# Another filling of TensorE's early gaps, another path for u, and another written order, in an attention-then-feed-forward kernel

## The chip, the cores and the metric

The kernel runs on one core of one Trainium2 chip. Times are device microseconds (us) of whole executions of the program; the traces are single executions taken by the hardware profiler. The engines are named as in the profile: PE is TensorE (PEld its weight loads), ACT is ScalarE, DVE is VectorE, POOL is GpSimd, SP is SyncE, which here does nothing but start transfers (DMAs). A name with a q, such as SPq, is the engine's instruction queue.

## The reference

Two layers follow one another. The first is a linear attention with a decaying state, for 4 batches, 8 heads, 768 time steps and 48 values per head; the second is a feed-forward block without a nonlinearity.

```
for t in range(S):                                   # S = 768
    cur   = einsum('bhd,bhe->bhde', u * k_t, v_t)
    y_t   = einsum('bhd,bhde->bhe', r_t, state + cur)
    state = w_t[..., None] * state + einsum('bhd,bhe->bhde', k_t, v_t)
x   = y as (B*S, H*D)                                # 3072 x 384
out = ((x @ w1) * (x @ w2)) @ w3 @ w_out             # w1, w2: 384 x 1024; w3: 1024 x 1024; w_out: 1024 x 384
```

Inputs and output are float32; the matrix products run in bfloat16.

## The kernel before, in words

**Attention.** The 768 steps of each batch are cut into 6 chunks of 128 steps, which makes 24 chunks, numbered n = 0 to 23. `load(n)` brings w, k, r and v of a chunk from HBM, four transfers of 192 KB on SP's queue, into tiles with 8 buffers each. `att(n)` lists the steps of a chunk. `ln` (ACT) takes the logarithm of w; `cs` (two matmuls) forms cumulative sums in PSUM; `ex` (ACT) takes exponentials; `krt` (DVE) scales k and r by them; `tr` and `trs` transpose the result, with PE and an ACT copy for chunks 0 to 10, with a transposing DMA on SP's queue for chunks 11 to 23 (`kr_dma=11`). `vb` turns v into bfloat16; `kv` (PE), `pc`, `ts`, `st`, `sb` carry the state to the next chunk. `m` (PE) forms the 128 by 128 products per head, `mb` (DVE) masks them. `uk1`, `uk2` (POOL), `ds` (DVE) and `yd` (POOL) make the term with u. `y` (PE) and `yb` (DVE) make the output; `yt` (PE) and `xt` (ACT) lay it down transposed in the tile xT.

**u.** `ld_u` loads the 384 values of u into one row; `ub` is a float32 matmul of a row of ones with it, so that all 128 rows hold u; `uc` copies that to the tile u_bc, which `uk1` of every chunk reads.

**Feed-forward.** Chunks are gathered into blocks of 1 to 4 (`blocks`), 512 columns at most. For block j and each eighth fi of the 1024 columns, `a{j}.{fi}` and `b{j}.{fi}` are three matmuls each, `as` (ACT) copies a out of PSUM and `ab` (DVE) multiplies. The matrix w3 @ w_out is computed on the chip: `wt` transposes an eighth of w3 on PE, `wm` multiplies it with w_out. `o{j}.{t}` is then eight matmuls per chunk, `os` copies it out, `st` stores it. The weights arrive in seven pieces by POOL's queue (w1.0, w2.0, w1.1, w2.1, wo, w3.0, w3.1), each issued when the step named in `triggers` is done; w3.0 and w3.1 are needed by the first and the fifth `wt`.

**The order.** All steps are handed to a planner (`Plan`). It keeps a list of costs of its own, lets each engine take the ready step that can start first, breaks ties by a rank (the place in the list, shifted by `nudge`), and writes out one fixed order per engine; each engine runs its instructions strictly in that order. `lead` and `every` say how far the attention chunks stand ahead of the feed-forward parts in the list, `early` how many blocks' a and b stand ahead of the w3 part. The planner also notes where PE would stand idle before 30 us by its own times, and `keep_busy` puts matmuls of a zero tile (`busy`) ahead of the step there; they write to a PSUM bank that the step overwrites.

In the profile nearly all instructions carry line 186, the helper that records them, so they are found by their tiles.

Of the kernel before, what the change touches and what calls it, by code (L numbers as in the profile page):

```python
# [12 lines left out]

NEVER = 999
TUNE = dict(
    blocks=[1, 2, 3, 3, 3, 4, 4, 4],
    early=1,
    triggers=["uk20", "uk11", "uk21", "uk22", "uk22", "uk22", "uk22"],
    lead=5, every=4.0,
    v_act=5, s_act=NEVER, d_pool=NEVER, y_dma=NEVER, kr_dma=11, ahead=2.0, fill=30, nudge={}, st_act=5,  # L20
)


class Plan:
# [133 lines left out]
    def run(self):  # L158
        windows = []
        for _ in range(6):  # L160
            order, new, start, end = self._pass(windows)
            if new == windows:
                break
            windows = new
        self.start, self.end = start, end
        self.fill, at = {}, 1.2
        for n in order:
            if self.steps[n]["eng"] == "PE" and start[n] < TUNE["fill"]:
                gap = start[n] - at - 0.15
                self.fill[n] = max(0, int(gap / (0.43 if start[n] < 9 else 0.22)))  # L170
                at = start[n] + self.steps[n]["length"]
        for n in order:
            self.steps[n]["fn"]()

# [16 lines left out]
def kernel(  # L191
# [20 lines left out]
    pe, act, dve, pool, sp = (InOrder(tc, e) for e in (nc.tensor, nc.scalar, nc.vector, nc.gpsimd, nc.sync))  # L212
# [3 lines left out]
    C = 128  # L216
# [35 lines left out]
    u_bc = consts.tile([C, H, D], F32)  # L252
    u_row = consts.tile([1, DM], F32)
    ones_r = consts.tile([1, C], F32)
    busy = consts.tile([C, TB], BF)
# [34 lines left out]
    plan = Plan()  # L290
    plan.buffers(w_in=NIN, kr_in=NIN, v_in=NIN, lw=NS, krt=NS, v_bf=3, uk=2, ds=2, yd=3,
                 trs=3, mbf=2, ts=2, st=2, sb=NS, y_bf=3, a_sb=3, o_sb=3, xT=3, abT=3, w3T=2, f=3)
    T = {}

    def keep_busy(step, t):
        for _ in range(plan.fill.get(step, 0)):
            pe.matmul(t, lhsT=busy[:, 0:C], rhs=busy, start=True, stop=True)

    def pair(step):
        t = (g01, g23)[plan.found[step] // 2]  # L300
        keep_busy(step, t[:, 0, :])
        return t

    def bank(step):
        i = plan.found[step]
        t = (g01, g23, g4)[i // 2][:, i % 2, :]
        keep_busy(step, t)
        return t
# [4 lines left out]
    def load(n):  # L313
        b, c = divmod(n, NC)

        def src(ap):
            return ap[b, :, c * C:(c + 1) * C, :].rearrange("h t d -> t h d")

        def ld_w():
            T["w_in", n] = inp.tile([C, H, D], F32, tag="w_in", name="w_in")  # L320
            sp.dma_start(T["w_in", n], src(w))

        def ld_k():
            T["kr_in", n] = inp.tile([C, 2, H, D], F32, tag="kr_in", name="kr_in")
            sp.dma_start(T["kr_in", n][:, 0], src(k))

        def ld_r():
            sp.dma_start(T["kr_in", n][:, 1], src(r))

        def ld_v():  # L330
            T["v_in", n] = inp.tile([C, H, D], F32, tag="v_in", name="v_in")
            sp.dma_start(T["v_in", n], src(v))

        plan.add(f"ld_w{n}", "SP", 0.57, ld_w, take=["w_in"], rows=1024)
        plan.add(f"ld_k{n}", "SP", 0.57, ld_k, take=["kr_in"], rows=1024)
        plan.add(f"ld_r{n}", "SP", 0.57, ld_r, needs=[f"ld_k{n}"], rows=1024)
        plan.steps[f"ld_r{n}"]["needs"] = []
        plan.add(f"ld_v{n}", "SP", 0.57, ld_v, take=["v_in"], rows=1024)
# [191 lines left out]
    def ffn_ab(j, fi):  # L530
# [4 lines left out]
        def half(nm, w_):  # L535
            t = T[nm, j, fi] = ps_f.tile([P, TB], F32, tag="f", name=nm)
            keep_busy(f"{nm}{j}.{fi}", t)
            for di in range(DI):
                pe.matmul(t[:, 0:N], lhsT=w_[:, di, fi * P:(fi + 1) * P], rhs=T["xT", j][:, di, 0:N],
                          start=(di == 0), stop=(di == DI - 1))  # L540
# [66 lines left out]
          free=[f"wm{fi}"])  # L607


    load(0)  # L610
    plan.add("ld_u", "SP", 0.5, lambda: sp.dma_start(u_row, u.rearrange("h d -> (h d)")[None, :]), rows=20)

    def ub():
        T["ub"] = bank("ub")[:, 0:DM]
        pe.matmul(T["ub"], lhsT=ones_r, rhs=u_row, start=True, stop=True)

    plan.add("ub", "PE", 0.9, ub, needs=["ld_u"], bank=1, lag=0.3)
    plan.add("uc", "ACT", 0.45, lambda: act.copy(u_bc.rearrange("t h d -> t (h d)"), T["ub"]),
             needs=["ub"], free=["ub"])
    for n in range(1, NU):  # L620
        load(n)
# [2 lines left out]
    for g in range(2):  # L624
        for nm, dst, ap in (("w1", w1_bf, moe_w1), ("w2", w2_bf, moe_w2)):
            cols = slice(g * FH * P, (g + 1) * FH * P)
            pieces.append((f"{nm}.{g}", dst[:, :, cols], ap[:, cols], 2.8))
    pieces.append(("wo", wo_bf, moe_w_out, 6.0))
    for g in range(FI // W3G):
        rows = slice(g * W3G * P, (g + 1) * W3G * P)  # L630
# [24 lines left out]
    lead, every = TUNE["lead"], TUNE["every"]  # L655
# [38 lines left out]
```

## Time and profile before

| what | us |
|---|---|
| 13 runs, median | 186.53 |
| 13 runs, lowest and highest | 183.35, 189.33 |
| the profiled execution, whole time | 183.84 |
| its span, first to last instruction | 182.1 |
| PE busy within the span | 169.3 |
| DVE, ACT, POOL busy | 126.4, 107.2, 90.1 |

The span is what the trace shows; 1.74 us of the profiled execution's 183.84 us lie around it. The profiled execution is among the fastest of the runs, 2.69 us below their median. A line of a timeline gives start, duration, engine, line, operation, output<-input, shape and count; in brackets stands how long the engine was idle before and what ended that. Matmuls overlap in the pipeline, so durations of several matmuls in one line can overlap with the next line's; the time that a group takes from PE is the distance between starts.

### The profile page before, as it was taken

To read this page: it belongs to the slowest core of one execution; us is meant where nothing else is said; L and a number is where in the kernel's file an instruction comes from. 1 tells how busy PE (TensorE), PEld (TensorE's weight loads), DVE (VectorE), ACT (ScalarE), POOL (GpSimd) and SP (SyncE) were. 2 spreads that over 40 slices of the span, in tenths; PEclk is the share of its full clock that TensorE was granted. 3 is DMA by queue.
4 is the path that set the end of the run, shared out by engine and by line. 5 is a ranking of instruction groups with operands and counts; after the bars stand their busy time and mean duration, and the time that the engine had idled before them with its cause. 6 is when DMAs were issued, how large, how long until landed. Compare 5 with 4: busy or idle time off the path is not lost.

```text
span 182.1 us, 4449 instructions
## 1 busy us (share of the span) xinstructions
PE 169.3 (93%) x1658; PEld 101.5 (56%) x1667; DVE 126.4 (69%) x220; ACT 107.2 (59%) x220; POOL 90.1 (49%) x136
## 2 busy tenths in 40 slices
PE   5996898878999998999999999999999999999992
PEld 1443465755676665665666666565556544554451
DVE  7265664654687985898799969958996798804510
ACT  3355534741567886978857675776666666345431
POOL 4167998700536793759674663476265636000000
PEclk9999999999999999999999999999999999999999
DMA  6999999999999999999989999999999997131013
GB/s 117 190 187 204 220 207 173 197 204 205 181 199 166 195 171 224 206 175 203 197 195 205 152 238 212 157 223 244 189 203 230 213 214 102 30 130 43 4 50 123
DMA packets 120744, 31.76 MB, mean 174 GB/s; under 512 B 114065, under 2 KB 119698, under 8 KB 120722
## 3 DMA queue, kind: packets, MB, share of 16 engines
q1 hardware_dynamic: 115298, 24.65, 81.3%
q0 software_dynamic: 3696, 4.46, 14.5%
q10 hardware_dynamic: 1728, 2.36, 3.8%
q8 instruction: 13, 0.21, 0.5%
q14 instruction: 9, 0.07, 0.1%
HBM read 27.79 MB, written 4.72 MB: 179 GB/s over the span
## 4 chain that ended last, share of the span: by engine, by line
PE 70%; DMA 11%; issue 6%; POOL 6%; DVE 4%; ACT 1%; POOLq 0%; ACTq 0%
PE g L186 19%; PE o_ps L186 17%; PE a L186 14%; PE b L186 13%; DMA w_bf<-in_moe_w_dram 9%; PE wm L186 5%; DMA trs<-krt 3%; POOL uk L186 2%; PE wt L186 2%; POOL sbd L186 1%; POOL w_bf L186 1%; DVE mbf L186 1%; ACT trs L186 1%; POOL v_bf L186 1%; DVE krt L186 1%
## 5 line engine op out<-in xcount | busy, mean ns | idle before, releaser
L186 PEld LDWEIGHTS <-w_bf 128*128 128x128 bf16 x448 | 37.9, 97 | 26.8 <-DMA w_bf<-in_moe_w_dram 1.8
L186 DVE TENSOR_TENSOR abT<-a_sb,b 128x384 bf16<-128x384 f32 (+3 forms) x64 | 34.8, 551 | 14.0 <-ACT a_sb L186 7.2
L186 ACT COPY a_sb<-a 128x384 f32<-128x384 f32 (+3 forms) x64 | 30.6, 479 | 20.2 <-PE a L186 18.0
L186 PE MATMUL a<-xT,w_bf 128*128 128x384 bf16 (+3 forms) x187 | 41.1, 324 | 0.8 <-ACT a_sb L186 0.2
L186 PE MATMUL b<-xT,w_bf 128*128 128x384 bf16 (+3 forms) x191 | 41.4, 325 | 0.1
L186 PE MATMUL o_ps<-w,abT 128*128 128x384 bf16 x192 | 34.5, 326 | 0.0
L186 POOL TENSOR_TENSOR yd<-v_bf,ds 128x384 bf16<-128x384 bf16 x24 | 19.9, 828 | 26.1 <-DVE ds L186 18.4
L186 DVE TENSOR_TENSOR mbf<-g,mask 128x1024 bf16<-128x1024 f32 x24 | 29.3, 1219 | 4.5 <-PE g L186 4.3
L186 POOL TENSOR_TENSOR uk<-kr_in,u_bc 128x384 f32<-128x384 f32 x24 | 23.9, 997 | 13.3 <-DMA kr_in<-in_k_dram 10.0
L186 ACT ACTIVATE g<-g 128x768 f32<-128x768 f32 (+1 forms) x44 | 22.1, 507 | 13.8 <-PE g L186 12.0
L186 DVE TENSOR_TENSOR krt<-kr_in,g 128x768 bf16<-128x768 f32 x24 | 22.8, 949 | 3.8 <-ACT g L186 3.8
L186 POOL TENSOR_TENSOR uk<-uk,kr_in 128x384 f32<-128x384 f32 x24 | 23.9, 997 | 1.4
L186 PEld LDWEIGHTS <-abT 128*128 128x128 bf16 x192 | 18.0, 98 | 11.4
L186 ACT COPY o_sb<-o_ps 128x384 f32<-128x384 f32 x24 | 11.5, 480 | 12.4 <-PE o_ps L186 12.2
L186 DVE TENSOR_TENSOR y_bf<-g,yd 128x384 bf16<-128x384 f32 x24 | 13.3, 554 | 4.8 <-POOL yd L186 3.1
L186 PE MATMUL g<-busy 128*128 128x512 bf16 x40 | 12.9, 435 | 3.6 <-DVE busy L186 1.3
L186 PEld LDWEIGHTS <-trs 48*128 48x128 bf16 (+1 forms) x272 | 10.6, 95 | 9.7 <-issue 4.2
L186 DVE TENSOR_REDUCE ds<-uk 128x8 f32<-128x384 f32 x24 | 13.0, 547 | 2.8 <-POOL uk L186 2.8
L186 PEld LDWEIGHTS <-krt 128*64 128x64 bf16 (+1 forms) x248 | 9.8, 107 | 9.2 <-issue 3.6
L186 ACT COPY trs<-g 128x1024 bf16<-128x1024 bf16 x11 | 11.1, 1013 | 5.7 <-PE g L186 5.6
L186 ACT COPY xT<-g 128x384 bf16<-128x384 bf16 x24 | 11.6, 482 | 4.9 <-PE g L186 2.7
L186 ACT ACTIVATE lw<-w_in 128x384 bf16<-128x384 f32 x24 | 12.6, 525 | 2.8 <-DMA w_in<-in_w_dram 2.8
(108 smaller groups left out, 179.8 us busy)
## 6 DMA issues: line engine op xcount, KB each, us to landing
w_in<-in_w_dram SPq DMA_DIRECT2D x24, 192.0 KB, 4.5
kr_in<-in_k_dram SPq DMA_DIRECT2D x24, 192.0 KB, 4.3
kr_in<-in_r_dram SPq DMA_DIRECT2D x24, 192.0 KB, 4.5
v_in<-in_v_dram SPq DMA_DIRECT2D x24, 192.0 KB, 4.3
out_dram<-o_sb SPq DMA_DIRECT2D x12, 192.0 KB, 3.2
out_dram<-o_sb ACTq DMA_DIRECT2D x12, 192.0 KB, 1.9
w_bf<-in_moe_w_dram POOLq DMA_DIRECT2D x2, 1024.0 KB, 18.2
w_bf<-in_moe_w_dram POOLq DMA_DIRECT2D x4, 384.0 KB, 6.2
```

The lines of the kernel that those rows point to most:

```text
L186: return self.tc.keep_in_program_order(f(*a, **k))
```

## The change

Four things change.

- **The zero matmuls.** Before, the planner put whole matmuls of 512 columns into a gap, one per 0.43 us before 9 us and one per 0.22 us after. Now it works out a number of columns, 1200 per us before 9 us and 1800 per us after, and emits pieces of 512 columns and one remainder of at least 64. The count starts at 0.5 us in place of 1.2, and before 9 us each PE step is taken as twice its listed length.
- **u.** `ld_u` moves from SP's queue, where it stood fifth, to ACT's queue, where it stands ahead of the first `ln`. `ub` gets a rank that puts it first on PE; `uc` moves from ACT to DVE, ahead of the first `krt`.
- **The written order.** `blocks`, `early`, `triggers`, `lead`, `every`, `v_act` (from which chunk ACT does `vb`) and `nudge` get other values, and so the planner writes another order on every engine.
- **Planner costs** of `ub` change from 0.9 (lag 0.3) to 0.7 (lag 0.6).

```diff
 TUNE = dict(
-    blocks=[1, 2, 3, 3, 3, 4, 4, 4],
-    early=1,
-    triggers=["uk20", "uk11", "uk21", "uk22", "uk22", "uk22", "uk22"],
-    lead=5, every=4.0,
-    v_act=5, s_act=NEVER, d_pool=NEVER, y_dma=NEVER, kr_dma=11, ahead=2.0, fill=30, nudge={}, st_act=5,
+    blocks=[2, 2, 2, 2, 4, 4, 4, 4],
+    early=2,
+    triggers=["uk20", "vb2", "vb2", "uk12", "uk13", "uk13", "uk13"],
+    lead=2, every=3.4,
+    v_act=6, s_act=NEVER, d_pool=NEVER, y_dma=NEVER, kr_dma=11, ahead=2.0, fill=30, nudge={'xt23': -36, 'kv9': 25, 'kv12': 51, 'yb5': 17}, st_act=5,
 )
...
-        self.fill, at = {}, 1.2
+        self.fill, at = {}, 0.5
         for n in order:
             if self.steps[n]["eng"] == "PE" and start[n] < TUNE["fill"]:
-                gap = start[n] - at - 0.15
-                self.fill[n] = max(0, int(gap / (0.43 if start[n] < 9 else 0.22)))
-                at = start[n] + self.steps[n]["length"]
+                gap = start[n] - at
+                cols = int((gap - 0.05) * 1200 if start[n] < 9 else (gap - 0.15) * 1800)
+                self.fill[n] = [512] * (cols // 512) + [c for c in [cols % 512] if c >= 64]
+                at = start[n] + self.steps[n]["length"] + (self.steps[n]["length"] if start[n] < 9 else 0)
...
-        for _ in range(plan.fill.get(step, 0)):
-            pe.matmul(t, lhsT=busy[:, 0:C], rhs=busy, start=True, stop=True)
+        for cols in plan.fill.get(step, []):
+            pe.matmul(t[:, 0:cols], lhsT=busy[:, 0:C], rhs=busy[:, 0:cols], start=True, stop=True)
...
+    plan.add("ld_u", "ACT", 0.5, lambda: act.dma_start(u_row, u.rearrange("h d -> (h d)")[None, :]), rows=20)
     load(0)
-    plan.add("ld_u", "SP", 0.5, lambda: sp.dma_start(u_row, u.rearrange("h d -> (h d)")[None, :]), rows=20)
...
-    plan.add("ub", "PE", 0.9, ub, needs=["ld_u"], bank=1, lag=0.3)
-    plan.add("uc", "ACT", 0.45, lambda: act.copy(u_bc.rearrange("t h d -> t (h d)"), T["ub"]),
+    plan.add("ub", "PE", 0.7, ub, needs=["ld_u"], bank=1, lag=0.6, rank=-20)
+    plan.add("uc", "DVE", 0.45, lambda: dve.tensor_copy(u_bc.rearrange("t h d -> t (h d)"), T["ub"]),
              needs=["ub"], free=["ub"])
```

## The prediction

> **What bounds the kernel now.** First the page: the busy line and the slices.
>
> ```profile
> PE 169.3 (93%) x1658; PEld 101.5 (56%) x1667; DVE 126.4 (69%) x220; ACT 107.2 (59%) x220; POOL 90.1 (49%) x136
> ...
> PE   5996898878999998999999999999999999999992
> ...
> DMA  6999999999999999999989999999999997131013
> ```
>
> PE looks like the bound, but the DMA engines are as full as PE from the second slice to the 33rd, about 4.6 to 150 us. The stage that decides must show which of the two the other waits for. So next the waits in the window 95 to 152 us and ACT's timeline in it:
>
> ```profile
> POOL uk L186 <- DMA kr_in<-in_k_dram: 10.0, 7, 4.6
> ...
> ACT lw L186 <- DMA w_in<-in_w_dram: 0.9, 2, 0.7
> ```
>
> ```profile
> 117.77 0.52 ACT L186 ACTIVATE lw<-w_in 128x384 bf16<-128x384 f32 x1
> 122.72 0.52 ACT L186 ACTIVATE lw<-w_in 128x384 bf16<-128x384 f32 x1 [0.25 <-DMA w_in<-in_w_dram]
> 130.38 0.53 ACT L186 ACTIVATE lw<-w_in 128x384 bf16<-128x384 f32 x1
> 135.43 0.52 ACT L186 ACTIVATE lw<-w_in 128x384 bf16<-128x384 f32 x1
> 142.05 0.52 ACT L186 ACTIVATE lw<-w_in 128x384 bf16<-128x384 f32 x1 [0.68 <-DMA w_in<-in_w_dram]
> 148.43 0.52 ACT L186 ACTIVATE lw<-w_in 128x384 bf16<-128x384 f32 x1
> ```
>
> These are `ln` of chunks 18 to 23. In the record of landings each w of these chunks lands at most 0.1 us before its `ln`; chunks 6 to 11 had 2 to 4 us to spare. From about chunk 15 (w used at 99.41) the attention lives from hand to mouth: (148.43 - 99.41) / 8 = 6.13 us per chunk. PE needs less per chunk: a and b 2.60 (16 groups of 0.65 for 4 chunks), o 1.30, and attention 1.56 (cs 0.33, kv 0.35, y 0.38, m 0.33, yt 0.17, from distances of starts), 5.46 in all. PE is full only because it works off parts left from earlier. The end, from the timeline of all engines:
>
> ```profile
> 151.03 0.95 DVE L186 TENSOR_TENSOR krt<-kr_in,g 128x768 bf16<-128x768 f32 x1
> 152.04 2.45 SPq L186 DMA_TRANSPOSE trs<-krt  x1
> 156.69 0.40 PE L186 MATMUL g<-trs 48*128 48x128 bf16 x8
> 162.93 0.81 PE L186 MATMUL a<-xT,w_bf 128*128 128x512 bf16 x2
> 173.29 5.36 PE L186 MATMUL o_ps<-w,abT 128*128 128x384 bf16 x32
> ```
>
> Chunk 23 sets it: its r lands at 150.5, `krt` runs at 151.03, the transposing DMA takes 4.60 us (152.04 to 156.64, in the chain), `m` starts at 156.69, and from there PE's order is fixed: yt22, the four o of block 6, y23 and yt23 between them, 6.24 us; a and b of block 7, 10.36; four o, 5.40; last copy and store, 3.41. 156.69 + 25.41 = 182.1.
>
> **The written order, at the front.** Before, 3 chunks of a and b stand ahead of the first `wt`; now 4 do (two blocks of two). One chunk is 16 groups of three 128-column matmuls, 0.167 us each by the rows at 24.17 and 24.33: 2.67 us of PE work that moves from behind the w3 wait into it. The wait, from the chain:
>
> ```profile
> 25.66 15.77 DMA w_bf<-in_moe_w_dram
> 41.47 0.63 PE wt L186 x8
> ```
>
> PE stood idle 1.54 us before that `wt`. POOL's queue issues the seven pieces at 12.48, 16.43, 19.86, 23.94, 24.74, 25.66 and 26.40. In the new order w1.0 stands ahead of the first v_bf, w2.1, w2.0 and w1.1 stand together, and wo and w3 follow after `uk1` of chunk 3. I take w3.0 as landing 0.5 us earlier: the three late pieces are issued closer together, but they land one after another and share the engines with loads. Bounds: 2.95 earlier (all of POOL's wait for u_bc, below), 0.9 later (one issue more ahead of it). Sum for PE at 41 us: 2.67 + 0.5 = 3.2 us ahead.
>
> That lead is not worth 3.2 us at the end. Total traffic is unchanged (same loads, same 13 transposes, 12 stores on SP and 12 on ACT), and the DMA engines were never idle, so chunk 23 lands about when it did. PE being ahead only runs dry sooner in the 95 to 150 us stretch: 8 chunks times (6.13 - 5.46) = 5.4 us that PE now fills with old work. What is late next is the transfer stream. **Worth 0**; if this cover is gone, -3.2.
>
> **The written order, at the tail.** Before, between `kv` of chunk 22 and `cs` of chunk 23 stands only `y` of 21 (148.53, 148.88, 149.26). In the new PE order b6.2 and a6.3 stand there too: 2 x 0.65. `cs` 23 was ready at 148.95 (end of `ln`) and waited 0.31. Cost between 0 (kv22 not late) and 1.3; I take 0.65, half, because kv22 itself follows a landing (v of 22, 147.4). It goes straight through ex, krt, the transpose and m to the end. nudge of xt23 saves nothing: its copy ended at 161.79 and the fourth o of block 6 held PE to 162.93 anyway. **+0.65**.
>
> **u.** The front, from the timeline:
>
> ```profile
> 3.63 0.90 SPq L186 DMA_DIRECT2D u_row<-in_u_dram  x1
> 8.13 0.92 PE L186 MATMUL g<-u_row,ones_r 1*128 1x384 f32 x2
> 9.90 0.48 ACT L186 COPY u_bc<-g 128x384 f32<-128x384 f32 x1 [0.23 <-DVE ts__195 L186]
> 10.47 1.00 POOL L186 TENSOR_TENSOR uk<-kr_in,u_bc 128x384 f32<-128x384 f32 x1 [2.95 <-ACT u_bc L186]
> ```
>
> SP's queue gains 0.90 us, so the loads of chunk 1 can be issued at 3.67 in place of 4.57. The engines had the four loads of chunk 0 in flight until 7.0, so this is worth 0 to -0.9 on the stream; I take 0. The Trainium skill, "Trainium Kernel Development and Optimization", Key Constraints, speaks against this part: DMAs of SP, ACT and POOL run on the same 16 engines, another queue saves issue time alone. The 0.90 us row is that issue time, and by the rule, too, the sum gets no more than it.
>
> On ACT the issue stands behind the table load (0.80 to 2.08) and ahead of `ln` 0, which waits for w until 3.91: hidden. The landing of u is not shown; between 0.8 + 3.1 (w0's whole path) and 2.98 + 3.1. Then `ub` (0.92 here, up to 1.84 at the early half rate) stands ahead of `cs` 0, which started at 4.49: cs0 comes 0 to 3.4 us later, I take 1.3. Queued behind it are ex0, krt0, tr0 and the whole chain of chunk 0; `uc` on DVE (0.48) runs while cs0 and ex0 do. Against it POOL's `uk1` starts some 4 us sooner and takes the 2.95 us wait away; `vb` of chunk 0 now comes behind uk1, uk2 and a weight issue (1.00 + 1.00 + 0.93) on POOL and `kv` 0 waits for it. All this is PE-side work of the front, covered by the stream: **0**; uncovered, within -3 and +3.
>
> **Zero matmuls.** 49 with 25,088 columns become 66 with 26,001. Most stand in gaps. But where the gap is zero the remainder of a negative number is positive: 19 pieces (17 of 242 columns, one of 333, one of 315) stand between steps that follow each other closely. Five of 512 columns take 1.24 us at full rate (row at 28.18), 0.48 ns a column, so 19 x 0.12 = 2.3 us, 12 of them (1.4 us) within a and b of block 0. Cover: the wait for w3.0, in which PE had 1.54 us idle, less now. **0**; uncovered +2.3.
>
> For the half rate: weight loads of the first zero matmuls start at 1.66, 2.08, 2.51, 0.42 us apart; those at 28.18 take 0.25. Of real work only cs0 and tr0 ran before full rate, under 2 us together, so warming at once saves under 1 us of PE. The Trainium skill, "TensorE: Matmul & The Clock Gate", Part 1, speaks against the aim as well: it puts the ramp under 1% of a typical kernel's span.
>
> **Sum.** 183.84 + 0 + 0.65 = 184.5 on the profiled execution's scale. The runs' median lies 2.69 above it, and I keep that distance: 187.2, given as 187.0, since some of the spread of the runs may be late fronts that the PE lead would now absorb.
>
> **Rivals.**
> - *PE is the bound after all* (27%). For it: 14.87 to 15.00 of each 15 us busy between 75 and 150. Against it: the loads used on landing. Then 3.2 us come through less up to 0.65: 186.53 - 2.6 = 183.9, down to 183.0 if POOL's wait also counts in part.
> - *A transpose blocks the load queue* (25%, slower). SP issues in order; the new order puts the transposes of chunks 11, 14 and 19 ahead of a load each (w of 14, k of 16, v of 20) that stood before it. In this trace w of chunk 14 is issued at 83.24, its k at 87.82 and r at 91.30, with two transposes and three stores between; chunk 14's r lands 9.1 us after chunk 13's, against 6.13: about 2.8 us lost. One more such stand, 186.53 + 2.8 = 189.3. It decides from the point where a krt is later than the queue's earlier loads take to drain; attention stands less far ahead (lead 2 for 5), which makes it possible.
> - *The change doesn't do what it says*: zero matmuls still start at 1.25, when DVE's memset of `busy` ends, and PE stands before `ub` for u. Likely, and it costs nothing; it is inside the forecast.
>
> Forecast, the stream decides: 48%, own range 185.2 to 188.4. Bound for faster or slower is 1%, 1.9 us, about what a measurement of this kernel can tell from no change. The range takes in most of both rivals: 183.2 to 189.4.
>
> **What would show it.** Right: `ln` of chunk 23 within 1 us of 148.4; its distance to the end 33.7 +- 1; u_bc by 7 us; three or more us of PE idle spread over 45 to 155; first `wt` at 40 to 41.5. PE right as the bound: `ln` 23 near 145.5 and PE without gaps. Blocked queue: SP waiting for krt with `ln` 23 past 151. Wrong altogether: the first `wt` after 43, through late w pieces or a cold PE.

## The result and the profile after

| | before | after |
|---|---|---|
| median of the runs (lowest to highest) | 186.27 (183.18 to 189.33, 48 runs) | 187.33 (186.12 to 188.79, 11 runs) |
| ratio after / before, 95% interval | | 1.0169 [1.0132, 1.0205] |
| the profiled execution, its span | 183.84, 182.1 | 188.04, 186.3 |
| w3.0 lands | 41.4 | 40.3 |
| first `wt` | 41.47 | 44.59 |
| first `o` | 63.50 | 66.56 |
| `ln` of chunk 23 | 148.43 | 152.25 |
| block 7's `a` begins | 162.93 | 167.17 |

The change makes the kernel slower, by 1.06 us between the medians. The ratio leaves out runs that lie over 1.5% above the fastest of their kernel, which keeps 22 of the 48 widely spread runs of before and all of after, so it is larger than that of the medians (187.33 / 186.27 = 1.006; both are above 1), and for the same reason the medians are given beside the ratios below.

The page of the changed kernel, busy line and slices, to be held against the ones above:

```profile
PE 173.5 (93%) x1671; PEld 105.9 (57%) x1684; DVE 127.5 (68%) x221; ACT 105.9 (57%) x218; POOL 90.9 (49%) x137
...
PE   7898978999999899979999999999999999999992
...
DMA  6999999999999957989999899999999994121013
```

Counted from 0, a slice being 4.66 us: PE is fuller in slices 0 and 3 to 4, where zero matmuls stand and, up to 16.27 us, the clock is at half (below), and in 7 to 9, around the old wait for w3.0; it has an 8 and a 7 in slices 13 and 17 where it had 9s. DMA has a hole in slices 14 and 15 (65 to 75 us), a 5 and a 7. The waits in the window 95 to 152 us (engine, operation, what it waited for: us, times, longest) and ACT's timeline:

```profile
POOL uk L187 <- DMA kr_in<-in_k_dram: 1.7, 3, 0.7
```

```profile
114.93 0.53 ACT L187 ACTIVATE lw<-w_in 128x384 bf16<-128x384 f32 x1
120.06 0.53 ACT L187 ACTIVATE lw<-w_in 128x384 bf16<-128x384 f32 x1
...
145.97 0.52 ACT L187 ACTIVATE lw<-w_in 128x384 bf16<-128x384 f32 x1
152.25 0.53 ACT L187 ACTIVATE lw<-w_in 128x384 bf16<-128x384 f32 x1
```

POOL now waits 1.7 us for k where it waited 10.0, and none of these `lw` (chunks 17, 18, 22, 23) shows a wait for its w. The transfers are less late than before, and chunk 23 is nevertheless 3.8 us later. The end, from the timeline of all engines:

```profile
155.46 0.95 DVE L187 TENSOR_TENSOR krt<-kr_in,g 128x768 bf16<-128x768 f32 x1
...
160.84 0.40 PE L187 MATMUL g<-trs 48*128 48x128 bf16 x8
...
167.17 0.81 PE L187 MATMUL a<-xT,w_bf 128*128 128x512 bf16 x2
...
177.53 5.36 PE L187 MATMUL o_ps<-w,abT 128*128 128x384 bf16 x32
```

From `m` of chunk 23 to the end it takes 25.5 us, as before (25.4). So the loss arises earlier. PE's timeline at the first `wt`:

```profile
43.51 0.49 PE L187 MATMUL b<-xT,w_bf 128*128 128x256 bf16 x3
43.87 0.49 PE L187 MATMUL a<-xT,w_bf 128*128 128x256 bf16 x3
44.20 0.49 PE L187 MATMUL b<-xT,w_bf 128*128 128x256 bf16 x3
44.59 1.05 PE L187 MATMUL wt<-I,w_bf 128*128 128x128 bf16 x16
```

Before, PE idled 1.54 us here for w3.0. Now there is no wait: w3.0 has lain there since 40.3 and PE is 4.3 us late with its own work. The 4.2 us of the two spans are 3.1 us up to this point and 1.1 us from here to the end (186.3 - 44.59 = 141.7, against 182.1 - 41.47 = 140.6).

### The profile page after: what moved, and what is told of

Read it like the earlier page. It is cut to its first block, busy times and chain, and to the rows that moved or that the text cites. A ratio compares the mean times of both kernels' runs of the same rounds, so it can differ in the third digit from the quotient of the medians.

```text
span 186.3 us, 4494 instructions
## 1 busy us (share of the span) xinstructions
PE 173.5 (93%) x1671; PEld 105.9 (57%) x1684; DVE 127.5 (68%) x221; ACT 105.9 (57%) x218; POOL 90.9 (49%) x137
## 4 chain that ended last, share of the span: by engine, by line
PE 86%; DVE 8%; ACT 3%; issue 2%; DVEq 0%; ACTq 0%
PE g L187 29%; PE o_ps L187 17%; PE a L187 17%; PE b L187 17%; PE wm L187 5%; DVE mbf L187 2%; ACT trs L187 2%; DVE y_bf L187 1%; DVE krt L187 1%; DVE abT L187 1%; DVE w3T L187 1%; ACT g L187 1%; PE wt L187 1%; ACT xT L187 0%; ACT o_sb L187 0%
## 5 line engine op out<-in xcount | busy, mean ns | idle before, releaser
L187 PEld LDWEIGHTS <-w_bf 128*128 128x128 bf16 x448 | 39.3, 97 | 23.0 <-issue 0.4
L187 DVE TENSOR_TENSOR abT<-a_sb,b 128x256 bf16<-128x256 f32 (+1 forms) x64 | 35.0, 552 | 20.6 <-PE b L187 10.0
L187 ACT COPY a_sb<-a 128x256 f32<-128x256 f32 (+1 forms) x64 | 30.6, 480 | 25.1 <-PE a L187 23.1
L187 PE MATMUL b<-xT,w_bf 128*128 128x256 bf16 (+1 forms) x190 | 41.4, 325 | 0.2
L187 PE MATMUL a<-xT,w_bf 128*128 128x256 bf16 (+1 forms) x184 | 40.8, 323 | 0.8 <-issue 0.3
L187 ACT ACTIVATE g<-g 128x768 f32<-128x768 f32 (+1 forms) x44 | 22.3, 510 | 13.9 <-PE g L187 10.6
L187 PE MATMUL g<-busy 128*128 128x512 bf16 (+10 forms) x49 | 15.9, 418 | 5.4 <-ACT trs L187 2.2
```

The costliest lines, as they stand in the source:

```text
L187: return self.tc.keep_in_program_order(f(*a, **k))
```

## The experiments

Three theories were set against each other: PE's own work ahead of `wt` is late (by the remainder pieces, by the half clock, by the new order); the transfer stream decides, as forecast; a store or transpose blocks the queue of loads. Times below are "first `wt`, `ln` 23, span" of the profile, and the ratio to the kernel before with its interval; in brackets the medians of the run and of the kernel before in its session.

**The parts one at a time.** e1: the new counting of zero matmuls alone, on the kernel before.

```diff
...
-                gap = start[n] - at - 0.15
-                self.fill[n] = max(0, int(gap / (0.43 if start[n] < 9 else 0.22)))
+                gap = start[n] - at
+                cols = int((gap - 0.05) * 1200 if start[n] < 9 else (gap - 0.15) * 1800)
...
```

> The kernel before with the new zero matmuls alone; u's path and the written order stay as before. If the new filling is what made the front late (full TensorE clock at 16.3 us in place of 8.2), this kernel has it too: median 1 us or more above before, full clock after 11 us, first wt after 42 us. If the written order is the cause: within 0.5 us of before, wt at 41.5. By the recorded prediction (the stream of loads decides): 0.

Measured: 41.25, 150.37, 184.4; ratio 1.0065 [1.0018, 1.0112] (185.43 against 185.87, so by the medians no loss). The front is not later; `wt` still waits for w3.0. The clock is full from 4.86 us, earlier than in any profile of the two kernels (below). The span of the profile is longer because PE waits late in the kernel, 2.5 us in 95 to 150 us against 0.3 before. The longest of these waits:

```profile
PE g L187 <- DMA trs<-krt: 1.5, 1, 1.5
```

It is the one profile in which a transfer held PE so long there: where the stream is not the bound, it is not far behind.

e2: the changed kernel with the old counting (the diff above reversed).

> The changed kernel with the zero matmuls filled by the old rule; order and u's path stay new. If the filling is the cause: 2 us or more below the changed kernel (187.3), first wt at 41 to 42 us instead of 44.6. If the written order is the cause: 186.5 to 188, wt still at 44 or later. By the recorded prediction: as the changed kernel.

Measured: 43.05, 150.71, 184.8; ratio 1.0097 [1.0046, 1.0148] (186.62 against 185.87).

e7: the new order alone, on the kernel before.

```diff
-    blocks=[1, 2, 3, 3, 3, 4, 4, 4],
-    early=1,
-    triggers=["uk20", "uk11", "uk21", "uk22", "uk22", "uk22", "uk22"],
-    lead=5, every=4.0,
+    blocks=[2, 2, 2, 2, 4, 4, 4, 4],
+    early=2,
+    triggers=["uk20", "vb2", "vb2", "uk12", "uk13", "uk13", "uk13"],
+    lead=2, every=3.4,
```

(v_act and nudge too, as in the change.)

> The kernel before with the new values of TUNE alone; u's path and the zero matmuls stay old (the planner writes the order anew, with u in its old place). If the new order costs PE time by itself: first wt to first a of block 7 takes 122.5 us or more, against 121.4 before, though one chunk of a and b less is left after wt; the end 1 to 3 us above before. If the order is harmless and the front alone is at fault: that distance is 119 us and the end within 0.7 of before.

Measured: 45.53, 153.0, 188.5; ratio 1.0191 [1.0123, 1.0259] (190.04 against 186.89). With u on its old path the new triggers come late: w3 is issued at 30.61 (24.75 in the changed kernel) and lands at 45.5, as late as `wt`. But PE's last wait ahead of `wt` is for a `krt` of the attention, not for w3.0, so both are late here (the clock, too, was at half again from 17.75 to 21.16). From PE's timeline:

```profile
45.07 0.62 PE L186 MATMUL g<-I,krt 128*128 128x128 bf16 x8 [0.80 <-DVE krt L186]
45.53 1.07 PE L186 MATMUL wt<-I,w_bf 128*128 128x128 bf16 x16
```

e18: the new path of u alone, on the kernel before.

```diff
+    plan.add("ld_u", "ACT", 0.5, lambda: act.dma_start(u_row, u.rearrange("h d -> (h d)")[None, :]), rows=20)
...
-    plan.add("ld_u", "SP", 0.5, lambda: sp.dma_start(u_row, u.rearrange("h d -> (h d)")[None, :]), rows=20)
...
-    plan.add("ub", "PE", 0.9, ub, needs=["ld_u"], bank=1, lag=0.3)
-    plan.add("uc", "ACT", 0.45, lambda: act.copy(u_bc.rearrange("t h d -> t (h d)"), T["ub"]),
+    plan.add("ub", "PE", 0.7, ub, needs=["ld_u"], bank=1, lag=0.6, rank=-20)
+    plan.add("uc", "DVE", 0.45, lambda: dve.tensor_copy(u_bc.rearrange("t h d -> t (h d)"), T["ub"]),
```

> The kernel before with the new path of u alone (issue on ScalarE's queue, ub first on TensorE, copy on VectorE). Theory (the old order waits for w3.0, and the pieces of the weights hang on uk of POOL, so u_bc 5 us earlier brings w3.0 earlier until TensorE itself is late): first wt 0.5 to 1.5 us earlier at a like clock, ratio 0.990 to 0.998. Rival (the prediction's step, covered by the stream): ratio 0.998 to 1.002. The other rival (ub and cs wait for u, the front is late): ratio over 1.003.

Measured: 48.68, 154.85, 191.8; median 196.82 against 186.19, ratio 1.046 [1.0347, 1.0572]. By its number the last expectation holds, but `cs` does not wait for u (`cs` 0 at 4.38, 4.49 before); the loss comes later. u_bc is copied from 4.33 to 4.87, and the first three pieces of the weights, which the old triggers hang on `uk`, land at 12.9, 16.4 and 20.3 (18.1, 22.9, 26.4 before). The attention's loads come later: SP's issue of a k stands for 10.15 us from 33.09 (before: 9.34 from 27.12), and the v behind it goes out at 46.48 (43.93). That the earlier weights push them back, on the same DMA engines, is argued from these times. POOL's timeline of e18, and then PE's:

```profile
38.07 1.00 POOL L186 TENSOR_TENSOR uk<-uk,kr_in 128x384 f32<-128x384 f32 x1
47.03 0.50 POOL L186 CAST v_bf<-v_in 128x384 bf16<-128x384 f32 x1 [7.96 <-DMA v_in<-in_v_dram]
```

```profile
47.59 0.41 PE L186 MATMUL g<-v_bf,krt 128*64 128x48 bf16 x8 [2.49 <-POOL v_bf L186]
```

POOL stands 7.96 us for a v, PE 2.49 us behind it; the granted clock falls to half from 46.66 to 53.49; and SP's queue then stands from 66.55 to 74.44 behind a store that waits for the first `o` (71.38). So u's early arrival is no gain by itself. With the new order it is one: without it 1.019 (e7), with it 1.010 (e2). The parts do not add up, 1.0065, 1.019 and 1.046 alone against 1.017 together.

**The remainder pieces.** e3: the changed kernel without the remainders of negative gaps.

```diff
-                cols = int((gap - 0.05) * 1200 if start[n] < 9 else (gap - 0.15) * 1800)
+                cols = max(0, int((gap - 0.05) * 1200 if start[n] < 9 else (gap - 0.15) * 1800))
```

> The changed kernel without the 19 zero matmuls that the remainder of a negative number puts between steps without a gap; all else as in the changed kernel. If they are what PE lacks: 19 x 0.12 = 2.3 us of PE work less, 1.4 of it within block 0, so first wt at 42.5 to 43.2 in place of 44.6 and the end 1 to 2 us earlier (185.3 to 186.3). If the late clock or the order is the cause: wt at most 1.4 earlier and the end within 0.7 of 187.3. By the recorded prediction: 0.

Measured: 41.74, 149.41, 183.5; ratio 1.0048 [1.0007, 1.0088] (185.97 against 185.87). In the changed kernel's timeline of PE they look like this:

```profile
33.46 0.49 PE L187 MATMUL a<-xT,w_bf 128*128 128x256 bf16 x3
33.79 0.27 PE L187 MATMUL b<-busy 128*128 128x242 bf16 x1
33.89 0.49 PE L187 MATMUL b<-xT,w_bf 128*128 128x256 bf16 x3
34.22 0.27 PE L187 MATMUL g<-busy 128*128 128x242 bf16 x1
```

Each moves the next step by 0.10 (33.79 to 33.89). With full clock at about the same time (e3 at 8.97, e14 below at 7.71) `wt` comes 43.02 - 41.74 = 1.3 us earlier without them, and the span is 1.3 us shorter (184.8 and 183.5). PE's timelines, first of e14, then of e3:

```profile
43.02 1.05 PE L187 MATMUL wt<-I,w_bf 128*128 128x128 bf16 x16
```

```profile
41.74 1.05 PE L187 MATMUL wt<-I,w_bf 128*128 128x128 bf16 x16
```

This is the largest loss found that one line undoes.

**The bank of the zero matmuls.** They write to the bank of the step that they stand before, and so wait for whoever still reads it. From PE's timeline of the changed kernel:

```profile
9.68 0.58 PE L187 MATMUL g<-busy 128*128 128x512 bf16 x1 [1.10 <-ACT trs L187]
```

PE idled 1.10 us ahead of a zero matmul that was to fill the gap. e4 gives those before 18 us, by the planner's times, a bank of their own, on the kernel before; e11 does so on e3.

```diff
+    warm = ps_f.tile([P, TB], F32, tag="f", name="warm")
...
+        if plan.start[step] < 18:
+            t = warm
```

> The kernel before; its zero matmuls of the first 18 us write a PSUM bank of their own, so that none of them waits for the bank of the step that it stands before. If waits inside the filling let the clock fall back or rise late in some executions, PE is without a gap over 1 us up to 16 us, full clock comes by 8.5 us, and the runs lie closer together, median 184 to 185. If the clock plays no part: median within 0.7 of before and the same spread (183 to 189).

Measured: 40.12, 147.14, 180.7; median 186.38 against 185.87, ratio 0.9979 [0.9888, 1.007].

> The changed kernel without the 19 remainder pieces, and with the zero matmuls of the first 18 us writing a bank of their own. Against the run without the remainder pieces alone (185.97, wt at 41.7 with full clock at 9.0): if the waits of zero matmuls for a bank keep the clock low, full clock by 9 us again and median 0.3 to 1 us lower, 185 to 185.7; if not, within 0.4 of 186.0. By the constant distance seen in four runs of this order, the end of the span comes 141.7 to 141.8 us after the first wt.

Measured: 45.57, 153.21, 187.3, in a profile with the clock at half again from 25.69 to 32.52, just after PE had waited 3.42 us for a `krt` (1.4 in e3); ratio 1.0062 [0.9992, 1.0132] (187.41 against 187.49), against 1.0048 for e3. The bank alone gains nothing that can be measured. In e11 it may cost: 7 of its 12 runs have a mean clock of 0.991 or lower, 1 of e3's 12. Why is open.

**The transfer stream.** e5 (kernel before) and e6 (changed kernel) load no r, a quarter of the attention's loads; k stands in for it, so y is not the reference's.

```diff
-            sp.dma_start(T["kr_in", n][:, 1], src(r))
+            pass
...
-            pool.tensor_mul(t, t, T["kr_in", n][:, 1])
+            pool.tensor_mul(t, t, T["kr_in", n][:, 0])
```

(`krt` reads k twice in the same way.)

> The kernel before without the 24 loads of r: k is read in r's place, so a quarter of the attention's traffic is left out and all instructions of PE, ACT, DVE and POOL stay. If the stream of loads decides (the recorded prediction): about 24 x 1.05 us of traffic less, no ln waits for its load, the median falls by several us, to where PE alone ends. If PE decides in the kernel before: the lowest runs stay at 183 to 184, and only the upper half of the runs (186 to 188) comes down to them, median 183.5 to 184.5.

Measured: 43.39, 150.07, 184.8; ratio 0.9987 [0.9934, 1.004] (186.43 against 186.89).

> The changed kernel without the 24 loads of r, as in the run before it. If the stream decides: falls by several us, as the kernel before does. If PE decides in the changed kernel: 186 to 187.5, within 1 us of the changed kernel, and then 2 to 3.5 us above the kernel before without r.

Measured: 42.64, 150.30, 184.4; ratio 1.0086 [1.0037, 1.0134] (187.10 against 186.89). From the timelines of e6:

```profile
42.64 1.05 PE L187 MATMUL wt<-I,w_bf 128*128 128x128 bf16 x16
...
150.30 0.53 ACT L187 ACTIVATE lw<-w_in 128x384 bf16<-128x384 f32 x1
```

From `wt` to `ln` 23 it takes 107.66 us in e6 and 107.66 in the changed kernel: to the hundredth the same, with the DMA engines moving 134 and 175 GB/s in 45 to 95 and 95 to 150 us against 183 and 204. In e5 it is 106.68 against 106.96, although there each w of chunks 18 to 23 lands 1.3 to 2.4 us ahead of its `ln`, where the kernel before had at most 0.1 us. The stream does not decide when chunk 23 comes. PE is all but full meanwhile; the stretch 95 to 150 us in before, after and e6 (its length, then busy time and count of PE, PEld, DVE, ACT and POOL, granted clock, DMA share, GB/s):

```profile
95.00:150.00 55.00, 54.71 (x545) 31.92 (x549) 46.97 (x79) 36.69 (x79) 29.79 (x42) 1.00 1.20 206
```

```profile
95.00:150.00 55.00, 53.95 (x532) 30.89 (x536) 45.61 (x77) 35.83 (x76) 31.30 (x45) 1.00 1.24 204
```

```profile
95.00:150.00 55.00, 54.60 (x538) 30.18 (x535) 46.04 (x77) 35.59 (x74) 32.13 (x47) 1.00 0.90 175
```

e9 (before) and e10 (changed) do the opposite: `o` adds up seven of the eight products and leaves out the last, 24 x 0.163 = 3.9 us less of PE; the output is short of that term.

```diff
-            for fi in range(FI):
+            for fi in range(FI - 1):
...
-                          start=(fi == 0), stop=(fi == FI - 1))
+                          start=(fi == 0), stop=(fi == FI - 2))
```

> The kernel before without the last of the eight products of every o (the last eighth of the hidden columns is left out of the output): 24 matmuls of 384 columns, 24 x 0.163 = 3.9 us of PE work less, no transfer less. If PE decides: 2.6 to 3.9 us below before, and ln of chunk 23 comes 2 us or more earlier. If the stream decides: only the eight o behind m of chunk 23 count, 1.3 us, and ln of chunk 23 stays within 0.7 us.

Measured: 44.36, 152.41, 184.6 (the clock was at half from 44.88 to 48.29); median 185.34 against 187.49, ratio 0.9841 [0.9708, 0.9973].

> The changed kernel without the last of the eight products of every o, as in the run before it. If PE decides: 2.6 to 3.9 us below the changed kernel (183.4 to 184.7). If the stream decides: 1.3 us below (186.0).

Measured: 44.45, 151.20, 184.1; ratio 1.0014 [0.9964, 1.0065] (185.69 against 187.49). The medians fall by 2.2 us (e9) and 187.33 - 185.69 = 1.6 us of 3.9 (e10; the full kernel is from other sessions, and the median of the kernel before moved between 185.87 and 187.49 from session to session, so this is rough). From `wt` to `ln` 23 e10 takes 106.75, 0.9 less, though about two thirds of the products left out stand there, 2.6 us. So PE binds up to chunk 23, but other limits stand close behind it: e10's PE has 1.9 us of idle in 95 to 150 us, half of it waits for ACT's xT and DVE's state, and in e9 `ln` 23 waited 0.48 us for its w.

**The stores on SP's queue.** In the changed kernel the loads stood from 64.5 to 68.6. SP's timeline:

```profile
63.49 0.99 SPq L187 DMA_DIRECT2D w_in<-in_w_dram  x1
68.57 0.36 SPq L187 DMA_DIRECT2D out_dram<-o_sb  x1
69.03 0.37 SPq L187 DMA_DIRECT2D kr_in<-in_k_dram  x1
```

k of chunk 10 is behind the first store, which waits for the first `o` (66.56) and its copy. e8 gives all stores to ACT's queue.

```diff
-            (act if st_act else sp).dma_start(out3[lo + t_], T["os", j, t_])
+            act.dma_start(out3[lo + t_], T["os", j, t_])
```

> The changed kernel with its first 12 output stores issued on ACT's queue, where copies ahead of them are already done, in place of SP's, where loads stand behind them; written order otherwise the same. If the loads behind late stores (SP quiet from 64.5 to 68.6 us) make the end late: ln of chunk 23 falls from 152.3 to about 149, the end by 1.5 to 3 us. If PE decides: loads land earlier, SP has no gap over 3 us between 60 and 75, and the end stays within 0.7 of 187.3.

Measured: 45.23, 163.69, 197.8; ratio 1.0669 [1.0608, 1.0731] (198.45 against 186.89). From ACT's timeline:

```profile
69.50 0.80 ACT L187 ACTIVATE g<-g 128x768 f32<-128x768 f32 x1
79.10 0.38 ACTq L187 DMA_DIRECT2D out_dram<-o_sb  x1
79.58 0.48 ACT L187 COPY xT<-g 128x384 bf16<-128x384 bf16 x1 [9.28 <-DMA w_in<-in_w_dram]
```

ACT stood 9.28 us; its issue of the first store came only when a load of w had landed, and all of ACT's work was behind it. Why the store waited for that load is open. The question of the queue is not answered by this run; the next four answer it in part.

**The clock.** The trace records the granted clock from the moment at which it becomes full. Until then PE runs at half: the first zero matmuls of 512 columns start 0.42 us apart, later ones 0.22 (in the kernel before at 1.25 and at 28.18). (The PEclk row of a page and its mean clock count this first stretch as full, so they don't show it.) In the profile of the changed kernel the clock is full only from 16.27 us, in that of before from 8.19. Whether the filling does this, single profiles can't tell. So both kernels, unchanged, were profiled twice more, on one chip.

> The kernel before, unchanged, profiled once more. Theory (the filling itself makes the clock full late): full clock at 8.6 us or earlier, first wt at 40 to 42 us, span = first wt + 140.6 (+-0.3). Rival (the moment of full clock is chance, whatever the filling): full clock anywhere from 4 to 16 us, and the first wt later with it.

> The changed kernel, unchanged, profiled once more. Theory (the filling itself makes the clock full late): full clock after 12 us again, first wt at 44 to 45 us, span 185.7 to 186.7. Rival (chance): full clock anywhere from 4 to 16 us; with 8 to 9 us the first wt would stand at 42.6 and the span at 184.4. Both: span = first wt + 141.75 (+-0.1).

> The kernel before, a third profile. As for the second: by the theory full clock at 8.6 us or earlier; by the rival anywhere from 4 to 16 us.

> The changed kernel, a third profile. As for the second: by the theory full clock after 12 us; by the rival anywhere from 4 to 16 us, span following the first wt at 141.75.

| profile | clock full from | w3.0 lands | first `wt` | span | span - `wt` |
|---|---|---|---|---|---|
| before | 8.19 | 41.4 | 41.47 | 182.1 | 140.6 |
| e15, before | 13.51 | 44.3 | 44.31 | 186.4 | 142.1 |
| e13, before | 16.36 | 44.6 | 44.68 | 185.4 | 140.7 |
| e14, after | 7.71 | 39.6 | 43.02 | 184.8 | 141.8 |
| e16, after | 13.42 | 40.2 | 43.81 | 185.6 | 141.8 |
| after | 16.27 | 40.3 | 44.59 | 186.3 | 141.7 |

Between these two kernels it is chance: about the same three moments turn up in both. Only at a like clock can the two be compared: at 8 us the change costs 2.7 us, at 16 us 0.9 (in the pair at 13.5 us the clock of e15 fell once more). A late clock costs the kernel before 3.3 us (182.1 to 185.4) and the changed one 1.5 (184.8 to 186.3): before, the pieces of w3 hang on POOL's `uk` of chunk 2, which comes later, and w3.0 with it (issued at 28.85 for 25.66, landed at 44.6 for 41.4); now PE's own work is last. That fits the runs, those of before spread over 6 us and those of after over 2.7; further falls of the clock, below, add to the spread. PE's timelines of e14 and then of the first profile of after show the same instruction at full and at half clock:

```profile
7.54 0.68 PE L187 MATMUL g<-I,krt 128*128 128x128 bf16 x8
...
12.10 0.32 PE L187 MATMUL g<-lw,LTn_incl 128*128 128x384 bf16 x1
```

```profile
7.54 1.04 PE L187 MATMUL g<-I,krt 128*128 128x128 bf16 x8
...
13.32 0.53 PE L187 MATMUL g<-lw,LTn_incl 128*128 128x384 bf16 x1
```

The cs of chunk 1 comes 1.22 us later, `wt` 1.57, and that lasts to the end.

What stands ahead of the first `cs` makes a difference all the same, over all 20 profiles. Where PE runs seven or eight zero matmuls there and nothing else (e1 eight, e12 and e17 below seven), the clock is full from 4.86, 4.41 and 4.03 us. Where it runs five and then idles 0.9 us (before and six others), it is full from 7.5 to 16.4 us, and where `ub`, a matmul of one row, stands between zero matmuls (after and nine others), from 7.7 to 16.3. PE's timeline of e1:

```profile
1.26 3.54 PE L187 MATMUL g<-busy 128*128 128x512 bf16 x8 [1.26 <-DVE busy L187]
```

So in its one profile the new counting alone goes with an early clock, and with the new path of u ahead of `cs` the early clock is gone. Three profiles are few, and that `ub` is the reason is argued.

In e15 the clock fell to half once more, from 44.23 to 47.65, at the end of PE's wait for w3.0:

```profile
41.45 0.49 PE L186 MATMUL b<-xT,w_bf 128*128 128x256 bf16 x3
44.31 1.89 PE L186 MATMUL wt<-I,w_bf 128*128 128x128 bf16 x16 [2.37 <-DMA w_bf<-in_moe_w_dram]
```

From `wt` to the end it then takes 142.1, 1.4 to 1.5 more than in the other two profiles. The stores too: in e13, the kernel before, the DMA digit of slice 14 is 3 and SP's queue stands from 64.1 to 68.7 behind the first store, while in e14, the changed kernel with the early clock, no digit there is below 7. So the hole in the changed kernel's DMA row is not the order's work; it goes with a late PE, and e14 loses about the same after `wt` (141.8 against 140.6 and 140.7) without it.

**After `wt`.** e13 and e14 hold all 240 matmuls of a and b of this stretch, so they can be counted. From `wt` to block 7's `a` e14 takes 122.57, e13 121.55, 1.02 more. By kind (distances from start to start, idle time apart): a and b 43.67 against 45.78, 2.11 less, since one chunk more was done before; idle 3.00 against 1.05, 1.95 more; cs, y and yt 18.59 against 17.22, 1.37 more; the rest -0.2. PE's waits from 43 to 95 us of e14, then from 45 to 95 us of e13:

```profile
PE g L187 <- ACT trs L187: 0.9, 1, 0.9
PE g L187 <- DVE y_bf L187: 0.8, 1, 0.8
PE wm L187 <- DVE w3T L187: 0.7, 2, 0.3
PE g L187 <- DVE mbf L187: 0.2, 1, 0.2
```

```profile
PE g L186 <- DVE st__1261 L186: 0.5, 1, 0.5
PE wm L186 <- DVE w3T L186: 0.3, 1, 0.3
PE g L186 <- DVE y_bf L186: 0.2, 1, 0.2
```

With less of a and b left to put between, and attention less far ahead, PE meets the steps of the attention before ACT and DVE have done theirs. That the lead is the reason is argued, not shown by a run; the waits are. Why cs, y and yt take 1.37 us longer is open.

**A version with lower medians than both.** e12: the kernel before with the own bank of e4 and seven zero matmuls, in place of five, ahead of the first `cs`. e17 adds seven in the wait for w3.0.

```diff
+        self.fill["cs0"] = 7
```

> The kernel before with a bank of their own for the zero matmuls of the first 18 us and seven of them in place of five ahead of the first cs, so that PE has no gap from 1.25 to 8 us. If the spread of the runs of before (183 to 189) comes from the time of full clock: full clock by 8.3 us in every execution, lowest to highest within 2.5 us, median 183 to 184.5. If the spread has another source (late transfers in the second half): median 185.5 to 187 and the spread as before.

Measured: 40.78, 147.1, 181.3, clock full from 4.41; median 184.64 against 187.49, ratio 0.996 [0.9915, 1.0006].

```diff
-        self.fill["cs0"] = 7
+        self.fill["cs0"], self.fill["wt0"] = 7, 7
...
+            keep_busy(f"wt{fi}", t.rearrange("p g c -> p (g c)").bitcast(F32))
```

> The kernel before with the fillings in a bank of their own, 7 zero matmuls more ahead of the first cs, and 7 ahead of the first wt, in the wait for w3.0. Theory (the idle wait of 1.5 to 2.6 us there lets the clock fall in some runs, and a fall costs 1.5 us): median 1 to 3 us below the kernel before, highest run below 187.5, ratio 0.984 to 0.995. Rival (the fall at that place is chance, the wait has nothing to do with it): as without these 7, ratio 0.996, or up to 1.5 us worse where the 7 come in the way of wt.

Measured: 41.04, 147.53, 181.6, clock full from 4.03; median 183.39 (182.31 to 185.31) against 186.19 (183.19 to 188.72), ratio 0.9952 [0.9901, 1.0002]. The seven fill the wait, in PE's timeline:

```profile
39.00 1.67 PE L187 MATMUL wt<-busy 128*128 128x512 bf16 x7
41.04 1.07 PE L187 MATMUL wt<-I,w_bf 128*128 128x128 bf16 x16 [0.36 <-DMA w_bf<-in_moe_w_dram]
```

Both medians lie 2.8 us below the kernel before of their session and below the changed kernel's 187.33; the intervals of both ratios just reach 1, so that it is faster is likely but not shown. What falls most is the upper end (185.31 against 188.72 in e17's session, the lower ends 182.31 and 183.19), as an early clock would do; that the early clock is the cause is argued from their two profiles. The seven in the wait have no effect of their own that shows (2.80 against 2.85), and falls of the clock are not gone: 4 of e17's 12 runs have a mean granted clock of 0.991 or lower, which one stretch of 3.4 us at half makes, and 37 of 105 of the kernel before. That the idle wait brings the fall, the theory of that run, is not shown.

## Why the prediction was wrong, point by point

The time forecast, 187.0, is near the median of 187.33, and that is luck. On the scale of the profiles the sum gave 184.5 where 188.04 came, and the 2.69 us added to it stood for the time of full clock (below). The direction was wrong: the ratio of 1.017 lies beyond the bound of 1%, that of the medians, 1.006, above 1 but within it. And the case that was to hold, "the stream decides", does not.

- **What bounds the kernel: wrong, the first step.** It was read from `ln` starting as w lands, and PE's 5.46 us per chunk against 6.13 was taken for slack. It was none: PE was busy 54.71 of the 55 us from 95 to 150, the rest of each 6.13 us being other work in its fixed order. `ln` starting as w lands can be seen equally when the loads follow PE: SP issues in order, its buffers come free and its stores go out when PE's work is done (10.6 us of SP's waits in the kernel before end with a product `g` of PE). A first sign was in the unchanged kernel: in e13 `wt` is 3.2 us later than in the profile of before and `ln` 23 3.3 us later. The test is e5 and e6: removing a quarter of the loads moved `ln` 23, counted from `wt`, by 0.3 and 0.0 us.
- **The front, put at 0 as covered by the stream: the step that failed in the sum.** Of the 3.2 us that PE was to be ahead nothing came. The wait of 1.54 us was spent twice, as room for 2.67 us more of a and b and as cover for 2.3 us of remainder pieces. At a like clock `wt` is 43.02 - 41.47 = 1.55 later (1.3 of it are the remainder pieces, by e3), and nothing covers it: it comes through to the end whole. The sign named as "wrong altogether", a `wt` after 43, is what came, half through a cold PE (1.57 us) and half through PE's own work (1.55), not through late w pieces.
- **The remainder pieces:** found, with 2.3 us uncovered; measured 1.3. Each moves the next step by 0.10 and not by 0.12: at 28.18 the zero matmuls start 0.22 us apart, and the 1.24 us of five include the end of the last. The size was near, the 0 was wrong.
- **The zero matmuls and the clock:** that the "zero matmuls still start at 1.25" holds. That warming at once "saves under 1 us" was mis-sized: full clock came between 4.0 and 16.4 us over all profiles, and 8 us of that are worth 3.3 us in the kernel before. The Trainium skill, "TensorE: Matmul & The Clock Gate", Part 1, which was called as a witness against the aim, puts the penalty of the ramp below 1% of a typical span; here the step from 8.2 to 16.4 us alone moved the end by 3.3 / 182.1 = 1.8%. The distance of 2.69 us between profile and median, which was kept as a constant, fits this: the profiled run of before had an early clock (183.84), e13 with a late one took 187.16.
- **The order after `wt`:** not in the sum at all but for the tail. It costs 1.1 us, though 2.1 us of a and b had left this stretch.
- **The tail, +0.65:** from `ln` 23 to block 7's `a` 14.92 against 14.50, so +0.42, part of that 1.1.
- **u:** arrived early as told, and more so. ACT's queue issued it at 0.83, during the table load of 0.80 to 2.08 and not behind it; `ub` started at 3.07, `cs` 0 at 4.82 against 4.49 (+0.33, 1.3 taken), the first `uk` at 5.40 against 10.47. Its worth was not 0 but hung on the order: 4.6% lost with the old one (e18), and with the new one 1.010 against 1.019 without it (e2, e7). At the first `wt` it brought nothing: w3.0 came 1.1 us earlier and PE was not ready for it.
- **The rivals:** that the change doesn't do what it says was half right: the zero matmuls still start at 1.25, but that costs, since in the changed kernel PE is held up by more of them and no earlier at full clock. "PE is the bound after all" was right about PE and wrong about the sign, because its 3.2 us of lead did not exist. "A transpose blocks the load queue" did not decide, though its sign, `ln` 23 past 151, came: from 75 to 152 us SP waited for `krt` 2.5 us in the changed kernel and 6.2 in e14, and from `wt` to `ln` 23 both took the same (107.66 and 107.65). The long stand of the queue was behind a store, and in the kernel before as well.

The sum as measured, in spans: 182.1 + 1.55 (front at a like clock) + 1.57 (clock 8 us later) + 1.1 (after `wt`) = 186.3. The 1.57 us are chance and not the change's doing: its own part is 2.7 us at an early clock and 0.9 at a late one, and the 1.06 us between the medians lie between.

## What to carry to other kernels

A load that is used on landing does not show that loads are the bound; ask what released the load's issue, and whether a second profile with a later start shifts it. A wait on the path is cover for one thing only: add up all that is put ahead of it before any of it is called hidden. Where one profile is taken, look at the moment of full clock before comparing two kernels, and profile the unchanged kernel again before giving a front's difference to the change.

## What the runs showed of the hardware

- The granted clock starts at half and becomes full at a moment that varies from run to run of one program: 8.2, 13.5 and 16.4 us, with PE at work from 1.25 us on but idle for 0.9 us before 4.5. The earliest were 4.4 and 4.0 in the two profiles with seven zero matmuls (for five), in a bank of their own, ahead of the first `cs`, and 4.9 in e1 with eight; three profiles are few against such a spread.
- It falls again in stretches of 3.4 us (44.23 to 47.65 in e15), 6.8 (46.66 to 53.49 in e18) or 10.2 (76.69 to 86.93 in e8). In e15 the fall came at the end of a PE wait of 2.4 us, in e18 1.6 us into one of 2.5, in e9 0.5 us after one of 2.2; waits of 1.4 to 1.5 us at the same place brought none (before, e5, e12, e13). The Trainium skill, "TensorE: Matmul & The Clock Gate", Part 1, tells of free-running windows of about 3.4 us; the length agrees. Its figure of some 3.4 us of sustained work up to full clock agrees with e1, e12 and e17, 2.8 to 3.6 us from the first matmul, and not with the others.
- A zero matmul waits for its bank like any other (1.10 us for ACT's `trs` in the changed kernel at 9.68; in e4, where the zero matmuls have a bank of their own, none waits for `trs`), so it does not fill the gap that this wait makes.
- The issue of a transfer on ACT's queue went out at 0.83, at the start of ACT's table load of 1.28 us.
